# First-batch q and k pieces in one transfer each, adjacent heads in the halves of TensorE, and the last attention units spread 8, 8, 5 over the phases

## The chip, the cores and the metric

The kernel runs on one core of a Trainium2 chip. The metric is device time in microseconds (us), from the first to the last instruction of one execution. Each time quoted is the median of several executions. Ratios are computed otherwise: the mean time of one kernel's fast runs over the mean of the other's fast runs in the same rounds, so a ratio is not quite the ratio of two quoted medians. The interval behind a ratio is a 95% interval.

A run counts as slow when it is over 1.5% above the fastest of the same kernel; slow runs are in the medians but not in the ratios.

In the profiles PE is TensorE's matmuls, PEld its weight loads, DVE VectorE, ACT ScalarE, POOL GpSimd (it issues the loads) and SP SyncE (it issues the DMA transposes and the stores). PSUM is the memory that TensorE's results go to, in eight banks (`ps`).

## The reference

Windowed causal attention with a linear distance penalty feeds a two-matrix layer with a cosine gate. There are 8 batches (B), 8 heads (H), 576 tokens (S) and 64 values per head (D).

```python
scores = q @ k.transpose(0, 1, 3, 2) / sqrt(64)
rel = pos[:, None] - pos[None, :]
scores = where((rel >= 0) & (rel < 128), scores - slope[h] * rel, -1e9)
x = softmax(scores) @ v                    # -> 4608 tokens x 512
h = x @ w_in                               # 512 -> 2048
out = (h * cos(h)) @ w_out                 # 2048 -> 512
```

## The kernel before

The kernel works through nine chunks of 512 tokens, one per phase `c`. A phase issues the first product of its chunk (`moe1`: TensorE, cosine on ScalarE, multiply on VectorE), then some attention units for later chunks, then the second product (`moe2`). A unit is one pair of heads and 256 queries, or the tail of a batch. Nine units are a batch. The first nine run before the phases, and `QUOTA` says how many run in each phase after that: 9 + 9 + 9 + 12 + 12 + 12 + 9 = 72.

```python
NX = 8
xnat = [sb(f"xnat{i}", [128, 256]) for i in range(NX)]
...
QUOTA = [9, 9, 12, 12, 12, 9]
...
for c in range(NCH):                       # NCH = 9
    ...                                    # first product of chunk c
    n = QUOTA[c] if c < len(QUOTA) else 0
    attention(every[done:done + n], c)
    done += n
    ...                                    # next batches: load_v, load_nat, dma_transposes
    moe2(c)
```

A unit ends with a normalisation on VectorE, which writes a row buffer `xnat[n % NX]`, where `n` counts units. From there the rows go to `xT` by a transpose on TensorE if the next phase needs them, and otherwise by a DMA transpose that SyncE issues. The buffer is free when that transfer has landed. The first two batches use another pair of buffers (`xg`), which two units share.

```python
key = ("xnat", n % NX)
o = xnat[n % NX][:, :].rearrange("p (r x d) -> p r x d", r=2, x=2)
...
op("dve", ... o, U[:, :, :, 0:64], rv[...], ALU.mult ..., w=[("B", ub), key])
...
op("sp", [lambda e: e.dma_start_transpose(
    xT[:, pr, t0:t0 + 256].rearrange("p (r t) -> p r t", r=2), xnat[n % NX][:, :])],
   r=[("xnat", n % NX)], w=xkeys(pr, t0, 256), dma=f"x{n % NX}", occ=1250, lat=500)
```

Batches 0 and 1 bring q and k in rows and transpose them on TensorE. Batch 0 comes in two pieces (tokens 0 to 255, then 256 to 575), each in two transfers, because its heads stand four apart:

```python
def head(b, pr, x):
    return pr + 4 * x if b < BPE else 2 * pr + x
...
fns = [lambda e, y=y: e.dma_start(
    qB[which][:, y, c0:c0 + 64 * R],
    src[b, 4 * y:4 * y + 4, t0:t0 + 32 * R, :].rearrange(
        "k (s j) d -> s k (j d)", j=R)) for y in range(2)]
op("pool", fns, ..., occ=800 if b else 1260, lat=2900 if b else 170 * R)
```

`occ` and `lat` are assumed costs. A list schedule orders all instructions by them before anything is emitted. Each engine then runs its own list strictly in order.

The softmax here doesn't subtract the row's maximum and nothing guards it: scores larger than these inputs give would overflow.

## Time and profile before

| | the kernel before |
|---|---|
| time before the prediction, three runs | 324.82 us (323.61 to 326.19) |
| profile given at first | 1098.3 us span, TensorE at about a quarter of its speed |
| profile of the same kernel taken later (run `base`) | 323.9 us span |

### The profile page before, as it was taken

The numbers are of one execution on the slowest core, as the hardware profiler recorded it, in microseconds if no ns is written. First come the engines' busy times: TensorE is split into PE (matmuls) and PEld (weight loads), VectorE is DVE, ScalarE is ACT, GpSimd is POOL, SyncE is SP. The second block draws the span as 40 slices with busy tenths as digits, with TensorE's granted clock in tenths as the row PEclk, the third lists the DMA queues.
The fourth block names the chain that finished last, engine by engine and source line by source line (L and its number), as shares of the span: only waits on it lengthen the run. The fifth ranks groups of instructions, "written<-read, shape, count | busy, mean of one in ns | idle before, by whom it ended". The sixth has DMA issues, their size and how long they took to land.

```text
span 1098.3 us, 6162 instructions
## 1 busy us (share of the span) xinstructions
PE 1066.8 (97%) x2411; PEld 370.2 (34%) x2450; DVE 198.6 (18%) x420; ACT 209.5 (19%) x290; POOL 97.4 (9%) x127
## 2 busy tenths in 40 slices
PE   7999999999999999999999999999999999999998
PEld 4653342234223432343234422332222222222222
DVE  5220222112211222122212221311101110120000
ACT  5222212212222212121222121211101110110000
POOL 9300023011200120021000000000000000000000
DMA  9910249143901570185015000100000000000000
GB/s 156 181 13 0 46 52 85 29 38 42 73 10 15 72 50 8 21 83 65 3 31 70 17 0 10 33 8 0 10 10 19 0 10 19 10 0 20 19 28 20
DMA packets 144540, 37.82 MB, mean 34 GB/s; under 512 B 134272, under 2 KB 139392, under 8 KB 144512
## 3 DMA queue, kind: packets, MB, share of 16 engines
q0 software_dynamic: 99680, 18.36, 20.6%
q1 hardware_dynamic: 44832, 19.08, 7.3%
q8 instruction: 19, 0.31, 0.1%
q14 instruction: 9, 0.07, 0.0%
HBM read 36.70 MB, written 9.44 MB: 42 GB/s over the span
## 4 chain that ended last, share of the span: by engine, by line
PE 97%; issue 2%; POOL 0%; DMA 0%; DVE 0%; ACT 0%; POOLq 0%; ACTq 0%
PE ps L741 42%; PE ps L695 38%; PE ps L718 5%; PE ps L503 4%; PE ps L581 3%; PE ps L584 2%; PE ps L659 1%; PE ps L450 1%; PE ps L570 1%; PE ps L494 1%; PE ps L568 0%; DMA qrows<-in_q_dram 0%; POOL qrows L330 0%; POOL krows L330 0%; DVE xgroup L626 0%
## 5 line engine op out<-in xcount | busy, mean ns | idle before, releaser
L741 PE MATMUL ps<-w_outb,gT 128*128 128x512 bf16 x550 | 471.6, 1097 | 12.6 <-issue 11.6
L695 PE MATMUL ps<-xT,w_inb 128*128 128x512 bf16 x499 | 421.0, 1105 | 7.9 <-issue 7.9
L741 PEld LDWEIGHTS ps<-w_outb,gT 128*128 128x128 bf16 x576 | 115.7, 207 | 289.4 <-issue 289.4
L695 PEld LDWEIGHTS ps<-xT,w_inb 128*128 128x128 bf16 x512 | 111.9, 220 | 287.8 <-issue 277.6
L704 DVE TENSOR_TENSOR gT<-ps,cos 128x512 bf16<-128x512 f32 x128 | 87.4, 690 | 400.2 <-PE ps L741 200.9
L700 ACT ACTIVATE cos<-ps,halfpi 128x512 f32<-128x512 f32 x128 | 86.6, 687 | 349.4 <-PE ps L695 281.3
L533 ACT ACTIVATE p<-ps 128x768 bf16<-128x768 f32 (+1 forms) x64 | 55.9, 918 | 164.2 <-PE ps L503 150.7
L340 POOL DMA_DIRECT2D vp<-in_v_dram x40 | 33.8, 857 | 404.4 <-PE ps L584 356.4
L747 ACT ACTIVATE ob<-ps 128x512 f32<-128x512 f32 x26 | 15.5, 597 | 244.4 <-PE ps L741 226.5
L718 PE MATMUL ps<-xT,w_inb 128*128 128x256 bf16 x128 | 54.2, 684 | 0.0
L581 PE MATMUL ps<-vp,p 128*128 128x65 bf16 x256 | 53.1, 347 | 0.5 <-issue 0.5
L581 PEld LDWEIGHTS ps<-vp,p 128*128 128x128 bf16 x256 | 40.3, 181 | 24.1 <-issue 22.3
L549 DVE TENSOR_TENSOR p<-p,emask 128x768 bf16<-128x768 bf16 (+1 forms) x64 | 38.5, 615 | 54.6 <-ACT p L533 53.9
L503 PE MATMUL ps<-qt,kt 64*128 64x128 bf16 (+1 forms) x320 | 48.3, 508 | 0.0
L584 PE MATMUL ps<-vp,p 128*128 128x65 bf16 x192 | 46.2, 333 | 0.0
L503 PEld LDWEIGHTS ps<-qt,kt 64*128 64x128 bf16 x320 | 22.9, 160 | 46.9 <-issue 44.4
L624 DVE RECIPROCAL rec<-ps 128x4 f32<-128x4 f32 x64 | 8.3, 168 | 138.0 <-PE ps L584 138.0
L718 PEld LDWEIGHTS ps<-xT,w_inb 128*128 128x128 bf16 x128 | 25.4, 204 | 22.3 <-issue 22.0
L584 PEld LDWEIGHTS ps<-vp,p 128*128 128x128 bf16 x192 | 30.3, 171 | 7.7 <-issue 7.7
L350 POOL DMA_DIRECT2D knat<-in_k_dram x30 | 25.4, 901 | 74.4 <-DMA kt<-knat 73.1
L350 POOL DMA_DIRECT2D qnat<-in_q_dram x30 | 25.3, 887 | 7.0 <-DMA qt<-qnat 7.0
L749 DVE COPY ob<-ps 128x512 f32<-128x512 f32 x10 | 6.9, 692 | 66.4 <-PE ps L741 66.4
(56 smaller groups left out, 253.3 us busy)
## 6 DMA issues: line engine op xcount, KB each, us to landing
out_dram<-ob SPq DMA_DIRECT2D x36, 256.0 KB, 2.0
vp<-in_v_dram POOLq DMA_DIRECT2D x32, 128.0 KB, 4.6
qnat<-in_q_dram POOLq DMA_DIRECT2D x24, 128.0 KB, 4.1
knat<-in_k_dram POOLq DMA_DIRECT2D x24, 128.0 KB, 4.0
w_inb<-in_moe_w_in_dram POOLq DMA_DIRECT2D x4, 512.0 KB, 10.1
w_outb<-in_moe_w_out_dram POOLq DMA_DIRECT2D x4, 512.0 KB, 21.1
qrows<-in_q_dram POOLq DMA_DIRECT2D x1, 576.0 KB, 14.7
krows<-in_k_dram POOLq DMA_DIRECT2D x1, 576.0 KB, 16.5
```

What stands on the lines that cost most here:

```text
L340: op("pool", [lambda e, t=t, rows=rows: e.dma_start(vp[b % 2][0:rows, t, :, 0:64], v[b, :, 128 * t:128 * t + rows, :].rearrange("h p d -> ...
L350: fns.append(lambda e, t=t, rows=rows: e.dma_start(nat[which][0:rows, t, :, :], src[b, :, 128 * t:128 * t + rows, :].rearrange("h p d -> p ...
L503: ins = e.matmul(ps[:, banks[x], c0:c1], keys_ap(b, x, pr, kc), query_ap(b, x, pr, qb, 128 * nb), start=True, stop=True)
L533: op("act", lambda e: e.activation(P[i][:, :, lo:512], src_[:, :, lo:512], ACTF.Exp, scale=0.125), w=held + [("P", i)], occ=920 if G else ...
L549: op("dve", lambda e: e.tensor_tensor(P[i][:, :, lo:512], P[i][:, :, lo:512], EM[:, h0:h1 + 1:h1 - h0, lo:512], ALU.mult), r=[("P", i), (" ...
L581: ins = e.matmul(o, P[i][:, x, d0:d0 + 128], V[:, kc, h, 0:65], start=True, stop=not two)
L584: ins = e.matmul(o, P[i][:, x, p0:p0 + 128], V[:, kc - 1, h, 0:65], start=False, stop=True)
L695: op("pe", lambda e, kc=kc: e.matmul(ps[:, bank, :], w_in[:, kc, 128 * fc:128 * fc + 128], xT[:, kc, r0:r0 + CH], start=(kc == 0), stop=(k ...
L700: op("act", lambda e: e.activation(cosb[ci][:, :], ps[:, bank, :], ACTF.Sin, bias=halfpi[:, 0:1]), r=["halfpi"], w=[("B", bank), ("cos", c ...
L704: op("dve", lambda e: e.tensor_tensor(gT[gi][:, fc, :], ps[:, bank, :], cosb[ci][:, :], ALU.mult), r=[("cos", ci)], w=[("B", bank), ("g", ...
L718: op("pe", lambda e, i=i, fc=fc, kc=kc: e.matmul(ps[:, bank, 256 * i:256 * i + 256], w_in[:, kc, 128 * fc:128 * fc + 128], xT[:, kc, r0:r0 ...
L741: op("pe", lambda e, t=t, fc=fc, bank=bank: e.matmul(ps[:, bank, :], gT[gi][:, fc, 128 * t:128 * t + 128], w_out[:, fc, :], start=(fc == 0 ...
```

## The change

The intent: fewer transfers to issue at the start, so that TensorE gets its first pieces sooner; adjacent heads, so that one access pattern covers a piece and one tail mask and one kind of result buffer serve all batches; and phases with less attention.

```diff
-        QUOTA = [9, 9, 12, 12, 12, 9]
+        QUOTA = [9, 9, 12, 12, 8, 8, 5]
...
-        def head(b, pr, x):
-            return pr + 4 * x if b < BPE else 2 * pr + x
...
-            if b:
-                fns = [... one transfer ...]
-            else:
-                fns = [... two transfers, y = 0 and 1 ...]
-            op("pool", fns, w=piece_keys(which, b, n), dma=f"ld{which}{n}",
-               occ=800 if b else 1260, lat=2900 if b else 170 * R)
+            rows = bass.AP(src.tensor, src[b].offset + 64 * t0,
+                           [[64 * R, 32], [64 * S, H], [1, 64 * R]])
+            op("pool", [lambda e: e.dma_start(qB[which][:, :, c0:c0 + 64 * R], rows)],
+               w=piece_keys(which, b, n), dma=f"ld{which}{n}", occ=800, lat=161 * R)
...
-            if b < BPE:
-                key = ("xg", pr // 2, pr % 2)
-                o = xg[pr // 2][:, :, :, 64 * (pr % 2):64 * (pr % 2) + 64]
-            else:
-                key = ("xnat", n % NX)
-                o = xnat[n % NX][:, :].rearrange("p (r x d) -> p r x d", r=2, x=2)
+            key = ("xnat", n % NX)
+            o = xnat[n % NX][:, :].rearrange("p (r x d) -> p r x d", r=2, x=2)
```

Cut: the masks in head order, one tail mask instead of two, `2 * pr + x` for `head(...)` everywhere, and what follows from them in the transposes. With the quota, the phase c = 4 goes from 12 units to 8, c = 5 from 9 to 8, and c = 6 from none to 5.

The single transfer cannot be tried under the old pairing: a build of that failed, because its source then needs four dimensions ("Unable to balance aps with more than 3 dims"). That is why the pairing had to change with it.

More of the change, by code (lines that the diff above doesn't have):

```diff
@@ L266, in bass_alibi_sliding__then__act_gcu_kernel @@
         EM = sb("emask", [128, H, 512])
-        EMt = [sb(f"emtail{i}", [128, H, 128]) for i in range(2)]
-        xg = [sb(f"xgroup{i}", [128, 2, 2, 128]) for i in range(2)]
+        EMt = sb("emtail", [128, H, 128])
         NP = 4
@@ L324, in load_qk @@
             c0 = 64 * (t0 // 32)
-            if b:
-                fns = [lambda e: e.dma_start(
-                    qB[which][:, :, :],
-                    src[b].rearrange("(y k) (s j) d -> (k s) y (j d)", y=2, j=18))]
-            else:
-                fns = [lambda e, y=y: e.dma_start(
-                    qB[which][:, y, c0:c0 + 64 * R],
-                    src[b, 4 * y:4 * y + 4, t0:t0 + 32 * R, :].rearrange(
-                        "k (s j) d -> s k (j d)", j=R)) for y in range(2)]
-            op("pool", fns, w=piece_keys(which, b, n), dma=f"ld{which}{n}",
-               occ=800 if b else 1260, lat=2900 if b else 170 * R)
+            rows = bass.AP(src.tensor, src[b].offset + 64 * t0,
+                           [[64 * R, 32], [64 * S, H], [1, 64 * R]])
+            op("pool", [lambda e: e.dma_start(qB[which][:, :, c0:c0 + 64 * R], rows)],
+               w=piece_keys(which, b, n), dma=f"ld{which}{n}", occ=800, lat=161 * R)
         def load_v(b, order=range(NBLK)):
@@ L415, in masks @@
         def masks():
-            for h in (0, 4, 1, 5, 2, 6, 3, 7):
+            for h in range(H):
                 op("act", lambda e, h=h: e.activation(
@@ L420, in masks @@
                    table=0)
-                if h >= 4:
+                if h % 2:
                     op("dve", lambda e, h=h: e.tensor_copy(
-                        EM[:, h - 4:h + 1:4, 256:512], EM[:, h - 4:h + 1:4, 0:256]),
-                       r=[("EM", h - 4), ("EM", h)], w=[("EM", h - 4), ("EM", h)],
+                        EM[:, h - 1:h + 1, 256:512], EM[:, h - 1:h + 1, 0:256]),
+                       r=[("EM", h - 1), ("EM", h)], w=[("EM", h - 1), ("EM", h)],
                        occ=250, lat=330)
-            for i in range(2):
-                for x in range(2):
-                    hs = [head(BPE * i, pr, x) for pr in range(NPAIR)]
-                    op("dve", lambda e, i=i, x=x, hs=hs: e.tensor_copy(
-                        EMt[i][:, 4 * x:4 * x + 4, :].rearrange("p h (n f) -> p h n f", n=2),
-                        EM[:, hs[0]:hs[-1] + 1:hs[1] - hs[0], 0:256].rearrange(
-                            "p h (n f) -> p h n f", n=2)[:, :, :, 0:64]),
-                       r=[("EM", h) for h in hs], w=[("EMt", i)], occ=500, lat=580)
+            for x in range(2):
+                op("dve", lambda e, x=x: e.tensor_copy(
+                    EMt[:, 4 * x:4 * x + 4, :].rearrange("p h (n f) -> p h n f", n=2),
+                    EM[:, x:x + 7:2, 0:256].rearrange("p h (n f) -> p h n f", n=2)[:, :, :, 0:64]),
+                   r=[("EM", h) for h in range(x, H, 2)], w=["EMt"], occ=500, lat=580)
         def qk_transposes(b, which, n, part, banks):
@@ L460, in qk_transposes @@
                     :, :, t0:t0 + 32 * R].rearrange("p k (s j) -> p k s j", j=R)[:, :, :, j0:j1]
-                order = "p (j k s) -> p k s j" if b else "p (j s k) -> p k s j"
-                src_ = dst(i).rearrange(order, j=j1 - j0, k=NPAIR)
+                src_ = dst(i).rearrange("p (j s k) -> p k s j", j=j1 - j0, k=NPAIR)
                 w = 140 * (j1 - j0)
@@ L543, in mask @@
                     Pt[i][:, 0:1024], Pt[i][:, 0:1024],
-                    EMt[b >= BPE][:, :, :].rearrange("p h f -> p (h f)"), ALU.mult),
-                   r=[("Pt", i), ("EMt", int(b >= BPE))], w=[("Pt", i)], occ=610, lat=693, pri=1)
+                    EMt[:, :, :].rearrange("p h f -> p (h f)"), ALU.mult),
+                   r=[("Pt", i), "EMt"], w=[("Pt", i)], occ=610, lat=693, pri=1)
                 return
             lo = 0 if G else 128
-            h0, h1 = head(b, pr, 0), head(b, pr, 1)
+            h0, h1 = 2 * pr, 2 * pr + 1
             op("dve", lambda e: e.tensor_tensor(
                 P[i][:, :, lo:512], P[i][:, :, lo:512],
-                EM[:, h0:h1 + 1:h1 - h0, lo:512], ALU.mult),
+                EM[:, h0:h1 + 1, lo:512], ALU.mult),
                r=[("P", i), ("EM", h0), ("EM", h1)], w=[("P", i)],
@@ L564, in f @@
                             for k_ in range(NPAIR):
-                                h = head(b, k_, x)
+                                h = 2 * k_ + x
                                 o = ps[:, UB[x], 65 * k_:65 * k_ + 65]
@@ L574, in f @@
                         for x in range(2):
-                            h = head(b, pr, x)
+                            h = 2 * pr + x
                             o = ps[:, ub, 65 * (2 * rb + x):65 * (2 * rb + x) + 65]
@@ L604, in norm @@
                 rv = rc[0:64, 0:8].rearrange("p (x k) -> p x k", x=2)
-                o = (xt_[:, :].rearrange("p (x k d) -> p x k d", k=4, x=2) if b < BPE else
-                     xt_[:, :].rearrange("p (k x d) -> p x k d", k=4, x=2))
+                o = xt_[:, :].rearrange("p (k x d) -> p x k d", k=4, x=2)
                 op("dve", lambda e: e.reciprocal(rv, U[:, :, :, 64]),
@@ L650, in x_pe @@
             else:
-                kc = pr // 2 + 2 * (pr % 2) if b < BPE else pr
                 def f(e):
@@ L656, in f @@
                     for r in range(2):
-                        i = (xg[pr // 2][:, r, pr % 2, :] if b < BPE else
-                             xnat[n % NX][:, 128 * r:128 * r + 128])
-                        ins = e.transpose(dst[:, 128 * r:128 * r + 128], i, ident[:, :])
+                        ins = e.transpose(dst[:, 128 * r:128 * r + 128],
+                                          xnat[n % NX][:, 128 * r:128 * r + 128], ident[:, :])
                     return ins
                 t0 = S * b + 256 * G
-                o, i = xT[:, kc, t0:t0 + 256], dst
-                keys = xkeys(kc, t0, 256)
-                rk = ([("xg", pr // 2, 0), ("xg", pr // 2, 1)] if b < BPE else
-                      [("xnat", n % NX)])
+                o, i = xT[:, pr, t0:t0 + 256], dst
+                keys = xkeys(pr, t0, 256)
+                rk = [("xnat", n % NX)]
             op("pe", f, r=rk + ["ident"], w=[("B", bank)], occ=120, lat=290, pri=0)
```

## The prediction

> **What bounds the kernel now.** I read the page first (busy shares, the chain that ended last, the groups), then the timeline of the first 24 us and of the last 8, then half-microsecond stretches of the start with the DMA rate. The first thing to see is that the profile is not of an execution like the timed ones: its span is 1098.3 us, the timed runs took 324.82 us.
>
> ```profile
> span 1098.3 us, 6162 instructions
> ...
> PE 1066.8 (97%) x2411; PEld 370.2 (34%) x2450; DVE 198.6 (18%) x420; ACT 209.5 (19%) x290; POOL 97.4 (9%) x127
> ...
> DMA 9910249143901570185015000100000000000000
> ...
> L741 PE MATMUL ps<-w_outb,gT 128*128 128x512 bf16 x550 | 471.6, 1097 | 12.6 <-issue 11.6
> L695 PE MATMUL ps<-xT,w_inb 128*128 128x512 bf16 x499 | 421.0, 1105 | 7.9 <-issue 7.9
> L704 DVE TENSOR_TENSOR gT<-ps,cos 128x512 bf16<-128x512 f32 x128 | 87.4, 690 | 400.2 <-PE ps L741 200.9
> ```
>
> TensorE is busy 97%, and the matmul groups have next to no idle time before them. What pace it runs at is seen in the last microseconds of the timeline, from one weight load to the next:
>
> ```profile
> 1090.50 0.26 PEld L741 LDWEIGHTS ps<-w_outb,gT 128*128 128x128 bf16 x1 [0.58 <-issue]
> 1091.34 0.26 PEld L741 LDWEIGHTS ps<-w_outb,gT 128*128 128x128 bf16 x1 [0.58 <-issue]
> ...
> 1095.12 0.60 ACT L747 ACTIVATE ob<-ps 128x512 f32<-128x512 f32 x1 [12.69 <-PE ps L741]
> ```
>
> One matmul of 512 columns every 0.84 us is 0.61 columns per ns. The two matrix products need 1152 such matmuls (9 chunks x 64, twice; the first chunk's are cut in halves), which is 968 us at that pace. That cannot fit in 324.82 us, so the timed runs have a TensorE about four times as fast, although the record gives the granted clock as 1.00. I therefore use the trace for what does not depend on TensorE (issues, transfers, ScalarE, VectorE), and rescale TensorE by 4.
>
> Rescaled sum for a timed run: 1152 x 0.216 us (the pace of the TensorE page, below) = 249 us. The chain of waits gives lines 741, 695 and 718 together 84.2% of the span, and the other TensorE lines (scores, attention times values, transposes) 12.5%, or 137 us; less some 14 us that lie in the start, a quarter of the rest is 31 us. The start, until the first matmul of the first product, takes 23.7 us in the timeline, and the end (last copy and store) about 3.3 us. Together 307 us; some 18 us of 324.8 are left for switches, gaps at the ends of phases and waits for transfers. So TensorE bounds a timed run as well, at some 90%. ScalarE's 209.5 us and VectorE's 198.6 us, which I take as unchanged, are 64% and 61% of 324.8: beside TensorE, but not far off in phases with much attention.
>
> The start is where the engines wait. Its timeline:
>
> ```profile
> 1.34 1.24 POOL L330 DMA_DIRECT2D qrows<-in_q_dram  x2 [0.82 <-POOLq L856]
> 2.56 1.09 POOL L330 DMA_DIRECT2D krows<-in_k_dram  x2
> 3.60 0.27 POOL L384 MEMSET ident<- 128x128 bf16 x1
> 5.00 1.67 PE L450 MATMUL ps<-ident,qrows 128*64 128x128 bf16 x16 [5.00 <-DMA qrows<-in_q_dram]
> 5.68 1.12 POOL L330 DMA_DIRECT2D qrows<-in_q_dram  x2 [0.15 <-issue]
> 7.44 1.56 PE L450 MATMUL ps<-ident,krows 128*64 128x128 bf16 x16 [0.77 <-DMA krows<-in_k_dram]
> 7.81 4.35 POOL L340 DMA_DIRECT2D vp<-in_v_dram  x5
> 10.21 2.14 PE L450 MATMUL ps<-ident,qrows 128*64 128x128 bf16 x20 [1.21 <-DMA qrows<-in_q_dram]
> 13.39 2.15 PE L450 MATMUL ps<-ident,krows 128*64 128x128 bf16 x20
> 15.07 0.76 POOL L326 DMA_DIRECT2D qrows<-in_q_dram  x1
> ```
>
> TensorE waits for each of the four pieces in turn. GpSimd is busy issuing all that time, and the second pieces, the values and the weights stand behind the first issues. The stretches show that the transfers are not at their limit early on:
>
> ```profile
> 4.50:5.00 0.50, 0.00 (x1) 0.01 (x2) 0.00 (x0) 0.00 (x0) 0.35 (x2) 1.00 0.77 92
> 6.50:7.00 0.50, 0.17 (x2) 0.00 (x0) 0.40 (x2) 0.50 (x3) 0.50 (x2) 1.00 0.42 52
> 16.50:17.00 0.50, 0.50 (x9) 0.26 (x6) 0.00 (x0) 0.50 (x2) 0.50 (x2) 1.00 1.28 212
> ```
>
> The last number is GB/s landed: 92 and 52 around 5 and 7 us, against about 205 once the weights flow. From 8 to 57 us the queue is never empty.
>
> **What the Trainium skill says.** "TensorE: Matmul & The Clock Gate", section "Seeing it yourself", warns that the clock events are unreliable and that the gate has been seen stuck at a quarter; this trace agrees, 0.61 columns per ns beside a recorded 1.00. The same page, "Back-to-back issue gap", gives N/2.4 + 2.5 ns warm, 216 ns for 512 columns; the trace cannot confirm it, the timed total only fits it. "DMA: Bandwidth & Descriptors", "Rules for kernel authors", says to coalesce small transfers; the trace shows what that saves here in issue, 0.76 us for one three-dimensional load against 1.24 us for two. "ScalarE: Activation LUTs", "What ACT_TABLE_LOAD costs", gives about 1283 ns for the load plus a drain; the trace has 1283 ns in all of them.
>
> **The change part by part.**
>
> *One transfer per tensor and piece.* Eight issues of batch 0 become four. Each pair costs 1.24, 1.09, 1.12 and 1.11 us; one issue of the same three-dimensional kind costs 0.76 or 0.71 us (line 326, batch 1). I take 0.74: the constants and the second q piece start 0.86 us earlier (1.24 + 1.09 - 2 x 0.74), the values and all behind them 1.6 us earlier. It is not all gain: the first half of q now leaves with the second, at about 2.1 instead of 1.9 us, so the first piece lands between 0.4 us earlier and 0.3 us later than 5.00. The second k piece, now at 13.39, is the last wait of the start; I expect it 1.0 to 1.6 us earlier. From there on transposes, scores and exponentials are unchanged, and the queue from 8 us on is moved by about as much, so weights and batch 1 arrive earlier too. On the path: -1.3 us.
>
> *Heads (2k, 2k+1) in the halves.* The mask multiply reads two adjacent heads instead of two four apart: same elements, same 615 ns. Two copies of the tail mask of 369 ns go (0.74 us of VectorE), at about 13.2 us, when the first exponentials run: off the path, 0 to -0.1. The result of the first two batches no longer waits for two units to share a buffer, and rotates over eight buffers instead of two: fewer waits of transposes, -0.2. The eviction of batch 1's transposes reads with a step of 4 instead of 1 across rows, but runs over the same inner dimension: 0.
>
> *Attention 8, 8, 5 instead of 12, 9, 0.* The 21 units stay 21, in 11 groups both before (6 + 5) and after (4 + 4 + 3). There is one more pair of table switches, 2 x 1.28 us of ScalarE. In a phase of 12 units ScalarE has 16 x 0.69 (cosines) + 12 x 0.92 (exponentials) + 2 x 1.28 (tables) + about 3 x 0.6 (output copies) = 26.5 us, against TensorE's 2 x 13.8 + some 5 = 33. After the cosines, 12 exponentials, two tables and the copies need 15.4 us, plus the waits between groups; the second product and the attention give TensorE 13.8 + 5 = 19 us to fill them with. So 12 units are near the limit at the end of the phase, where 8 leave several us. I give this 0.5 to 1.5 us for the 12, and take back up to 0.5 for the extra phase with a table switch. On the path: -0.8 us.
>
> *Order.* Instruction order is set by a list schedule on assumed costs; new costs shuffle it everywhere. I give this no sign and 1 us.
>
> Sum: -1.3 - 0.3 - 0.8 = -2.4 us; 324.82 - 2.4 = 322.4 us, 0.7% less.
>
> **The rivals.** *Start hidden by the queue:* the first pieces are bound by transfer, not issue, and the weights and batch 1's values come no earlier. For it: the queue is full from 8 to 57 us, and the last quarter of w_out lands near 43 us, about when a fast TensorE would need it. Against it: 52 and 92 GB/s early. Time: 323.6. *Late attention costs:* the phase with 5 units puts two table loads and exponentials where TensorE had nothing but dense matmuls, and a gap of 1 to 2 us opens. For it: the phases after 5 have no waits now. Against it: 13.8 us of second product to fill with and only 5 x 1.02 + 2.56 = 7.7 us on ScalarE. Time: 325. *Phase ends cost more than I think:* up to 18 us are unaccounted for; if phases of 12 lose 3 to 4 us each, the change wins more. For it: ScalarE and VectorE above 60%. Against it: only one of the three such phases is thinned. Time: 319.5.
>
> **Range and chances.** The three runs before lie between 323.61 and 326.19, so a median moves by about 0.8 us by itself; the start adds 0.8, the phases 1.2, the order 1. In quadrature 1.9 us, so 8 in 10 is about +-2.5, stretched downward for the last rival: 319.2 to 324.9. Faster by over 2% needs under 318.3: 8%. Slower by over 2% needs over 331.3, for which nothing speaks: 2%.
>
> **What would show it.** Four issues of about 0.74 us for batch 0's q and k; the identity's memset near 2.8 instead of 3.60 us; waits of TensorE for the second pieces ending near 9 and 12 us; the first product's first matmul near 22.4 instead of 23.73 us; two table loads more; two tail-mask copies fewer; no late gap of TensorE in the seventh phase. If the second k piece lands later than 13 us, or one issue costs over 1 us, the first part is wrong. If the profile comes out slow again, its span says nothing of the gain, and only the start can be compared.

## More of the kernel before

The prediction shows the first profile. The second came with the experiments and is the one to compare. Its head, with busy time, share of the span and instructions of each engine:

```profile
span 323.9 us, 6162 instructions
...
PE 306.1 (94%) x2411; PEld 154.7 (48%) x2450; DVE 190.1 (59%) x420; ACT 202.7 (63%) x290; POOL 97.6 (30%) x127
...
PE   2699999999999999999999979999999999999995
```

TensorE (PE) bounds the kernel, as the prediction worked out from the slow profile (some 90%). The row of digits gives TensorE's busy tenths in 40 slices of 8.1 us. Apart from the start and the last slice it holds one 7, in the slice from 186 to 194 us. The slow profile could not show that one.

## The result

| | median of six runs | ratio |
|---|---|---|
| before | 326.10 us (323.61 to 327.63) | |
| after | 321.65 us (320.85 to 322.34) | 0.9872 (0.9828 to 0.9915) |

The kernel is 1.28% faster, about 4.2 us of 326.1. That is within 2%, as predicted, and 321.65 us lies in the predicted range. The gain is larger than the 2.4 us worked out, though: the kernel before also came out at 326.1 here, not 324.82. A later repeat gave 322.00 us against 325.72 (ratio 0.9899), so the gain is 3.3 to 4.2 us. Why it is larger is what the experiments are for.

The head of the page after, and the two costliest lines of the groups (line, engine, operation, output and input, count, busy time, mean ns, then idle time ahead of them and its releaser):

```profile
span 319.1 us, 6207 instructions
...
PE 306.3 (96%) x2450; PEld 152.9 (48%) x2450; DVE 187.5 (59%) x413; ACT 204.1 (64%) x297; POOL 95.8 (30%) x123
...
PE   2799999999999999999999999999999999999995
...
L714 PE MATMUL ps<-w_outb,gT 128*128 128x512 bf16 x576 | 138.8, 379 | 0.0
L668 PE MATMUL ps<-xT,w_inb 128*128 128x512 bf16 x512 | 116.8, 379 | 0.4 <-DVE xnat L604 0.3
```

TensorE is as busy as before, 306 us, in a span 4.8 us shorter, and the 7 in the middle of its row is gone. Line 714 is the old 741 (second product) and 668 the old 695 (first product). The mean of 379 ns is from start to modelled end, and matmuls overlap. The pace is read from the weight loads at the end, one line of the timeline (start, length, line, count):

```profile
312.05 3.34 PEld L714 LDWEIGHTS ps<-w_outb,gT 128*128 128x128 bf16 x16
```

The last of 16 loads takes about 0.1 us, so (3.34 - 0.10) / 15 = 0.216 us lie from one to the next. The fourfold TensorE that the prediction had to assume is there.

The start of the timeline, where each piece was to come earlier. Before (run `base`):

```profile
7.30 1.06 PE L450 MATMUL ps<-ident,krows 128*64 128x128 bf16 x16 [1.27 <-DMA krows<-in_k_dram]
...
9.95 1.28 PE L450 MATMUL ps<-ident,qrows 128*64 128x128 bf16 x20 [1.59 <-DMA qrows<-in_q_dram]
...
13.25 1.28 PE L450 MATMUL ps<-ident,krows 128*64 128x128 bf16 x20 [1.27 <-DMA krows<-in_k_dram]
...
19.94 0.61 PE L718 MATMUL ps<-xT,w_inb 128*128 128x256 bf16 x2
```

After:

```profile
1.33 0.83 POOL L321 DMA_DIRECT2D qrows<-in_q_dram  x1 [0.81 <-POOLq L829]
...
2.15 0.72 POOL L321 DMA_DIRECT2D krows<-in_k_dram  x1
...
2.87 0.22 POOL L371 MEMSET ident<- 128x128 bf16 x1
...
5.26 1.07 PE L434 MATMUL ps<-ident,qrows 128*64 128x128 bf16 x16 [5.26 <-DMA qrows<-in_q_dram]
...
6.54 1.07 PE L434 MATMUL ps<-ident,krows 128*64 128x128 bf16 x16 [0.21 <-DMA krows<-in_k_dram]
...
9.29 1.28 PE L434 MATMUL ps<-ident,qrows 128*64 128x128 bf16 x20 [1.69 <-DMA qrows<-in_q_dram]
...
11.62 1.28 PE L434 MATMUL ps<-ident,krows 128*64 128x128 bf16 x20 [0.30 <-ACT qt L448]
...
17.34 0.61 PE L691 MATMUL ps<-xT,w_inb 128*128 128x256 bf16 x4
```

Single issues cost 0.83 and 0.72 us, and the identity comes at 2.87 us. The first q piece is 0.3 us later (4.96 in `base`). The others are 0.76, 0.66 and 1.63 us earlier, and the first product starts 2.6 us earlier.

Part of this is not the issue but the transfer. These are half-microsecond stretches of the start (stretch, its length, busy time and count of TensorE, weight loads, VectorE, ScalarE, GpSimd, then granted clock, DMA share, GB/s). Before:

```profile
4.50:5.00 0.50, 0.04 (x2) 0.04 (x4) 0.00 (x0) 0.00 (x0) 0.35 (x2) 1.00 0.91 123
```

After:

```profile
4.50:5.00 0.50, 0.00 (x0) 0.00 (x0) 0.00 (x0) 0.22 (x1) 0.35 (x2) 1.00 1.26 205
```

A first piece is 8 heads x 256 tokens x 64 values x 2 bytes = 262,144 bytes. At 205 GB/s that is 1.28 us, and 1.28 us is also what lies between the first q and the first k piece now (5.26 to 6.54). Before it was 2.34 us.

To see where the rest went I kept an account from the trace. Every weight load stands for one matmul, and all 2450 are recorded. I added up the work ahead of each at the full-speed pace of its kind (0.216 us for 512 columns; scores, values and transposes likewise, 298.2 us in all) and subtracted it from the time at which the load started. What is left is time lost so far. "Start" is read after 14 us of work, in the first product, "fifth phase" at 165 to 170 us of work, in the phase c = 4, and "after it" at 180.

| time lost so far, us | start | fifth phase | after it | end |
|---|---|---|---|---|
| before (`base`) | 14.2 | 17.4 | 19.9 | 21.9 |
| after | 11.55 | 15.1 | 15.3 | 17.1 |
| difference | 2.6 | 2.3 | 4.6 | 4.8 |

So the gain of this pair of profiles comes from two places: the start, 2.6 us, and something in the fifth phase, 2.3 us. In the fifth phase before, the timeline has this. TensorE:

```profile
190.39 0.20 PE L581 MATMUL ps<-vp,p 128*128 128x65 bf16 x1 [1.05 <-DVE xnat L626]
...
193.10 0.19 PE L568 MATMUL ps<-vp,ptail 128*128 128x65 bf16 x1 [1.00 <-DVE xnat L626]
```

and VectorE:

```profile
189.91 0.42 DVE L626 TENSOR_TENSOR xnat<-ps,rec 128x256 bf16<-128x256 f32 x1 [1.28 <-DMA xT<-xnat]
191.38 0.42 DVE L626 TENSOR_TENSOR xnat<-ps,rec 128x256 bf16<-128x256 f32 x1 [1.04 <-DMA xT<-xnat]
```

and the chain of waits through that stretch (start, length, what):

```profile
183.96 7.39 DMA xT<-xnat
```

TensorE waits for VectorE, and VectorE waits to write a row buffer until the DMA transpose of the unit eight before has landed, 7.39 us after its issue. The landing is only half of the time for which the buffer was held. The two buffers had been written by 177.35 and 177.68 us, but SyncE, which issues in order, had the transposes of the next batch's q first:

```profile
175.88 4.83 SPq L359 DMA_TRANSPOSE qt<-qnat  x1
180.75 1.24 SPq L362 DMA_TRANSPOSE qt<-qnat  x1
182.12 1.17 SPq L682 DMA_TRANSPOSE xT<-xnat  x1
...
183.96 2.36 SPq L682 DMA_TRANSPOSE xT<-xnat  x1
```

So their own transposes were issued 4.8 and 6.3 us after the buffers were full and landed at 189.88 and 191.35 us: each buffer was held for 12.5 to 13.7 us. What issuing them ahead of q would bring, no run tried. VectorE's late write also frees the PSUM bank for TensorE's next values, and the masks of later units stand behind it in VectorE's list. Over the whole page the phase costs TensorE the 7 in its row. The DMA view of 170 to 190 us gives the same landing time for these transposes after the change as before (count, median us):

```profile
xT<-xnat SPq DMA_TRANSPOSE x3, 7.6
```

Only nobody waits for them there. Two of them landed at 186.62 and 186.87 us, and the units that write these two buffers next now come in the phase after. VectorE after, at the same units, without a wait:

```profile
204.36 0.76 DVE L604 TENSOR_TENSOR xnat<-ps,rec 128x256 bf16<-128x256 f32 x2
```

### The profile page after: what moved, and what is told of

It is laid out like the page before. It is cut to its first block, busy times and chain, and to the rows that moved or that the text cites.

```text
span 319.1 us, 6207 instructions
## 1 busy us (share of the span) xinstructions
PE 306.3 (96%) x2450; PEld 152.9 (48%) x2450; DVE 187.5 (59%) x413; ACT 204.1 (64%) x297; POOL 95.8 (30%) x123
## 4 chain that ended last, share of the span: by engine, by line
PE 90%; DMA 6%; POOL 1%; issue 1%; DVE 0%; ACT 0%; POOLq 0%; ACTq 0%
PE ps L714 40%; PE ps L668 35%; DMA qrows<-in_q_dram 6%; PE ps L486 5%; PE ps L564 3%; PE ps L691 2%; PE ps L567 2%; PE ps L434 1%; PE ps L632 1%; PE ps L477 1%; PE ps L551 1%; PE ps L553 1%; POOL w_inb L357 1%; POOL qrows L321 0%; POOL krows L321 0%
## 5 line engine op out<-in xcount | busy, mean ns | idle before, releaser
L714 PE MATMUL ps<-w_outb,gT 128*128 128x512 bf16 x576 | 138.8, 379 | 0.0
L668 PE MATMUL ps<-xT,w_inb 128*128 128x512 bf16 x512 | 116.8, 379 | 0.4 <-DVE xnat L604 0.3
L714 PEld LDWEIGHTS ps<-w_outb,gT 128*128 128x128 bf16 x576 | 53.7, 98 | 58.7 <-issue 1.9
L668 PEld LDWEIGHTS ps<-xT,w_inb 128*128 128x128 bf16 x512 | 47.2, 98 | 61.2 <-DVE gT L677 6.0
L604 DVE TENSOR_TENSOR xnat<-ps,rec 128x256 bf16<-128x256 f32 x64 | 24.4, 420 | 0.7 <-DVE rec L602 0.4
L486 PE MATMUL ps<-qt,kt 64*128 64x128 bf16 (+1 forms) x320 | 19.0, 243 | 0.7 <-ACT p L516 0.7
L602 DVE RECIPROCAL rec<-ps 128x4 f32<-128x4 f32 x64 | 8.2, 168 | 18.1 <-PE ps L567 17.8
L564 PEld LDWEIGHTS ps<-vp,p 128*128 128x128 bf16 x256 | 15.4, 97 | 7.0 <-issue 3.5
L564 PE MATMUL ps<-vp,p 128*128 128x65 bf16 x256 | 18.2, 193 | 0.2 <-DVE p L532 0.2
L486 PEld LDWEIGHTS ps<-qt,kt 64*128 64x128 bf16 x320 | 11.2, 95 | 12.4 <-issue 5.1
L567 PE MATMUL ps<-vp,p 128*128 128x65 bf16 x192 | 17.0, 193 | 0.0
L691 PE MATMUL ps<-xT,w_inb 128*128 128x256 bf16 x128 | 16.0, 273 | 0.3 <-ACT xT L641 0.3
L567 PEld LDWEIGHTS ps<-vp,p 128*128 128x128 bf16 x192 | 13.3, 97 | 0.6
## 6 DMA issues: line engine op xcount, KB each, us to landing
qrows<-in_q_dram POOLq DMA_DIRECT2D x1, 576.0 KB, 15.1
krows<-in_k_dram POOLq DMA_DIRECT2D x1, 576.0 KB, 17.1
```

The costliest lines, as they stand in the source:

```text
L486: ins = e.matmul(ps[:, banks[x], c0:c1], keys_ap(b, x, pr, kc), query_ap(b, x, pr, qb, 128 * nb), start=True, stop=True)
L564: ins = e.matmul(o, P[i][:, x, d0:d0 + 128], V[:, kc, h, 0:65], start=True, stop=not two)
L567: ins = e.matmul(o, P[i][:, x, p0:p0 + 128], V[:, kc - 1, h, 0:65], start=False, stop=True)
L604: op("dve", lambda e: e.tensor_tensor(o, U[:, :, :, 0:64], rv[:, :, :, None].broadcast_to([128, 2, 2, 64]), ALU.mult), r=[("rec", n % 2)], ...
L668: op("pe", lambda e, kc=kc: e.matmul(ps[:, bank, :], w_in[:, kc, 128 * fc:128 * fc + 128], xT[:, kc, r0:r0 + CH], start=(kc == 0), stop=(k ...
L714: op("pe", lambda e, t=t, fc=fc, bank=bank: e.matmul(ps[:, bank, :], gT[gi][:, fc, 128 * t:128 * t + 128], w_out[:, fc, :], start=(fc == 0 ...
```

## The experiments

**Theory A** (from the profiles): the gain is two separate things, the start and the row buffers of the phase with 12 units. **Rival B** (from the prediction): the phase term comes from ScalarE at the end of a phase, so more buffers do nothing. **Rival C**: the list schedule's new order does it, or a colder TensorE clock at the start. **Rival D**: the pairing of heads has its own share.

The first four runs shared one chip and took the change apart. The kernel before came out at 325.78 us there.

**`base`**: the kernel before, unchanged, as a control.

> The kernel before, unchanged: ratio 1.00. It is run for a profile in the fast state. My theory (start 1.3 us, phases 0.8 us): the first matmul of the first product starts about 1.3 us later than the 17.34 us of the changed kernel, and TensorE shows some idle time at the ends of the phases with 12 units, 0.5 to 1.5 us in the fifth. Rival (all of the gain at the start): TensorE is without gaps from 20 us on, as in the changed kernel, and the first product starts 3 to 4 us later. Rival (reshuffled order): start and phases look alike and the difference is spread over many small pieces.

Measured: 325.60 us, ratio 0.9961 (0.9916 to 1.0006). The control is 0.4% from 1 by itself, so a ratio that is under half a per cent from another is not read alone.

**`quota_alone`**: the kernel before with the new quota.

```diff
-        QUOTA = [9, 9, 12, 12, 12, 9]
+        QUOTA = [9, 9, 12, 12, 8, 8, 5]
```

> Only the units per phase are changed (8, 8, 5 for 12, 9), the loads and heads are those of before. My theory: 0.8 us faster, ratio 0.9975. Rival that all of the gain is at the start: 1.000. Rival that thick phases cost more: 3 us faster, 0.990.

Measured: 323.01 us, ratio 0.9910 (0.9862 to 0.9958), 2.6 us under the control by medians. The account shows no loss through the fifth phase (16.5 us before and after it, against 17.4 and 19.9 in `base`). Its start differs by 1.6 us from that of `base` though the code of the start is the same, so profiles of single executions scatter by that much there. The time is what the rival "thick phases cost more" gave (0.990), not the 0.9975 of the theory.

**`whole_old_quota`**: the changed kernel with the old quota.

```diff
-        QUOTA = [9, 9, 12, 12, 8, 8, 5]
+        QUOTA = [9, 9, 12, 12, 12, 9]
```

> The changed kernel with the old units per phase (12, 9): one transfer per tensor and the new heads alone. My theory: 1.6 us of start and heads remain, ratio 0.995. Rival that all of the gain is at the start: 0.987, the whole. Rival that thick phases cost more: 0.996 to 1.000.

Measured: 325.87 us, ratio 0.9979 (0.9929 to 1.0030). Everything but the quota is worth nothing by itself. The account says where it went: the start is 2.1 us better (12.05), and the fifth phase loses 4.4 us (15.4 to 19.8) instead of 2.5. The hole became one wait of 3 us. TensorE and VectorE:

```profile
188.93 0.24 PE L564 MATMUL ps<-vp,p 128*128 128x65 bf16 x1 [3.00 <-DVE p L532]
```

```profile
187.52 0.76 DVE L604 TENSOR_TENSOR xnat<-ps,rec 128x256 bf16<-128x256 f32 x2 [2.81 <-DMA xT<-xnat]
```

After it the granted clock is 0.64 from 188 to 190 us and 0.50 from 190 to 192, where `base` has 1.00, so this profile loses more than the length of the wait. Whether the wait brings the lower clock on, no run tested; without the wait (`old_quota_nx12`, below) it stays at 1.00. The earlier start brings TensorE to this place 3.4 us sooner (it runs dry at 185.93 instead of 189.34 us), while the first of the two transfers lands only 2.4 us sooner (187.50 instead of 189.88).

**`two_transfers`**: the changed kernel, but with two transfers for each piece of batch 0, still in the new pairing (alternate heads in the two halves).

```diff
+            fns = [lambda e, y=y: e.dma_start(
+                qB[which][:, y, c0:c0 + 64 * R],
+                bass.AP(src.tensor, src[b].offset + 64 * t0 + 64 * S * y,
+                        [[64 * R, 32], [2 * 64 * S, 4], [1, 64 * R]])) for y in range(2)]
...            # with occ=1260, lat=170 * R for batch 0
```

> The changed kernel with two transfers per tensor and piece for batch 0 again (each takes every second head), with the issue cost of before given to the schedule; new heads and new units per phase. My theory: it loses the 1.3 us of the start, ratio 0.991 where the whole change has 0.987. Rival that the transfers are hidden by the queue anyway: 0.987 as the whole. Rival that all of the gain is the one transfer: 1.000.

Measured: 323.45 us, ratio 0.9921 (0.9880 to 0.9963), within 0.5 us of `quota_alone`: the pairing of heads with its removed copies and buffers is worth nothing that can be seen here. Against the whole change (0.9872 and 0.9899, in other rounds), the two transfers cost 0.2 to 0.5%, some 0.7 to 1.6 us, though the intervals overlap. The start is back as it was: first pieces at 5.02 and 7.32 us, the second q piece at 10.00 us, 111 GB/s in the stretch from 4.5 to 5 us. So the faster landing belongs to the single transfer, not to the order of heads.

The next four runs, on another chip (kernel before 324.99 us), put theory A against its rivals.

**`base_nx12`**: the kernel before with 12 row buffers. The order of instructions on every engine is the same as with 8 (the traces agree).

```diff
-        NX = 8
+        NX = 12
```

> The kernel before with 12 buffers for the attention rows instead of 8; the order of instructions on every engine is the same. Buffer theory (in the fifth phase VectorE waits for a row buffer whose DMA transpose stands behind the transpose of keys): both holes of TensorE near 188 and 191 us, 2.7 us together, go; 2.7 us faster, ratio 0.992. ScalarE theory of the prediction (12 units are too much for ScalarE at the end of a phase): the holes stay, 1.000.

Measured: 322.80 us, ratio 0.9946 (0.9925 to 0.9968), somewhat less than the 2.7 us expected. This one number takes 2.2 us out of the kernel before by medians, without touching the quota, ScalarE's work or the order. VectorE at the same place:

```profile
189.31 0.76 DVE L626 TENSOR_TENSOR xnat<-ps,rec 128x256 bf16<-128x256 f32 x2
```

No wait stands ahead of it, and the account runs level through the phase (18.1, 18.2). Rival B falls: 12 units in a phase are not too many for ScalarE. One thing in the expectation is not exact. It says that the slow transposes stand behind the transposes of the keys. In the queue's own list they are issued earlier (183.96 us, the keys' at 186.76); it is the transposes of q that stand ahead of them. Around that time the transpose of q takes 9.8 us to land and v's loads 9.4 us, so all transfers are slow there. Which of them slows the others no run separated.

**`old_quota_nx12`**: the changed kernel with the old quota and 12 row buffers.

```diff
-        NX = 8
+        NX = 12
-        QUOTA = [9, 9, 12, 12, 8, 8, 5]
+        QUOTA = [9, 9, 12, 12, 12, 9]
```

> The changed kernel with the old units per phase and 12 row buffers; order of instructions the same as with 8. Buffer theory: the hole of 3.2 us near 185 us and the slow clock after it go, about 4.6 us in all, and the gain of the start becomes visible: ratio 0.987, as the whole change. ScalarE theory: 0.998 as with 8 buffers.

Measured: 321.51 us, ratio 0.9909 (0.9889 to 0.9929), short of the 0.987 of the buffer theory but far from the 0.998 of its rival. The new quota isn't needed once there are buffers. And against `base_nx12` on the same chip, 322.80 - 321.51 = 1.3 us is what the start (with pairing and order) is worth when the hole isn't there to eat it.

**`costs_alone`**: the kernel before with the new assumed costs, so only the order of instructions changes, on TensorE in 646 lines; the transfers stay two per piece.

```diff
-               occ=800 if b else 1260, lat=2900 if b else 170 * R)
+               occ=800, lat=161 * R)
```

> The kernel before, with only the assumed costs of the first loads set to the changed kernel's: the same transfers and units, but the list schedule orders the instructions anew (646 lines of difference on TensorE). Theory of transfers and buffers: within 0.4% of the kernel before, 0.997 to 1.003, as long as the hole in the fifth phase stays. Rival that reshuffled order made the gain: 0.990 or less.

Measured: 326.47 us, ratio 1.0043 (1.0015 to 1.0070). This order by itself makes the kernel slower by 1.4 us; its profile has a wait of its own of 1.64 us, until 119.46 us, for a transpose of k. So the new costs alone do not make the gain. The changed kernel's own order, which the pairing and the quota shape too, was not tried alone. An order can cost over a microsecond, and the 1.3 us of the start contain a change of order.

**`early_pieces`**: the changed kernel with the second pieces issued right after the identity, ahead of the rest of the constants (an iota and two selections).

```diff
         constants()                        # now only the identity and the memsets
         load_qk("q", q, 0, 1)
         load_qk("k", k, 0, 1)
+        distances()                        # iota and two selections
         load_v(0)
```

> The changed kernel with the second q and k pieces issued ahead of the distance constants (iota and two selects), behind the identity alone. The second q piece is issued at about 3.5 instead of 4.90 us. Theory that the start is bound by the issue of the pieces: it lands near 8 instead of 9.29 us, and 1.0 to 1.3 us are gained over the changed kernel, ratio 0.983. Rival that the transfers bound it by now: lands no earlier than 9 us, ratio 0.987.

Measured: 321.57 us, ratio 0.9897 (0.9869 to 0.9926), no different from the whole change. The issue came 1.5 us earlier and the piece 0.6 us later (9.29 in the whole change):

```profile
3.42 0.76 POOL L321 DMA_DIRECT2D qrows<-in_q_dram  x1
...
9.87 1.28 PE L437 MATMUL ps<-ident,qrows 128*64 128x128 bf16 x20 [2.17 <-DMA qrows<-in_q_dram]
```

From issue to use it takes 6.45 us instead of 4.39. From there on, then, the second pieces are bound by the transfer and not by the issue.

The last four runs, on a third chip (kernel before 325.72 us), tested the clock and looked for a better version. In the fast profiles TensorE is slow at the start though the record says 1.00: in `base`, matmuls of scores with values lie 54 to 56 ns apart up to 22.64 us and 29 from 22.73 on; in the profile after they are 29 apart from 13.59 us on. An earlier full clock was therefore a rival for the start's gain.

**`base_warm`** and **`whole_warm`**: the kernel before and the changed one with throw-away transposes of the identity ahead of TensorE's four waits for pieces (6, 12, 16, 14 and 14, 3, 17, 5), outside the schedule, so that the order is unchanged. Shown for the changed one:

```diff
+        WARM = {'q0': 14, 'k0': 3, 'q1': 17, 'k1': 5}
...
+                def pre(e):                # emitted ahead of the waits for batch 0's pieces
+                    for _ in range(WARM[f"{which}{n}"]):
+                        e.transpose(spare psum bank, ident[:, :], ident[:, :])
```

> The kernel before with throw-away transposes of the identity (6, 12, 16 and 14) ahead of TensorE's four waits for q and k pieces; all other instructions in the same order. Clock theory: in the kernel before TensorE runs at half rate until 16 to 22 us because it idles so much in the start; kept busy, it reaches the full rate by 9 us, the scores near 16 us go at 36 instead of 60 ns, and 1.5 to 2 us are gained: ratio 0.994. Rival (only the landings matter): 1.000, or slower by the throw-away work that outlasts a wait, up to 1.003.

> The changed kernel with throw-away transposes (14, 3, 17, 5) ahead of the same four waits. Clock theory: the full rate comes at about 8 instead of 13 us, which shortens the second pieces' transposes and the first scores: 0.5 to 1 us less than the changed kernel of the same call. Rival: the same time within 0.3 us.

**`whole_again`**: the changed kernel once more, as the control.

> The changed kernel once more, beside the others of this call: ratio 0.987 to 0.991.

Measured: `base_warm` 329.80 us, ratio 1.0046 (0.9988 to 1.0103), with three of six runs slow and left out of the ratio; `whole_again` 322.00 us, 0.9899 (0.9857 to 0.9941); `whole_warm` 322.29 us, 0.9903 (0.9865 to 0.9942). With the throw-away work TensorE was at its full pace (transposes 56 ns apart) by 9.8 us in `base_warm` and 7.8 in `whole_warm`, and the first product came no sooner: at 19.81 us (19.94 in `base`) and at 18.45 (17.34 to 18.40 in three profiles of the changed kernel, one of them with 12 buffers). The times alone would not tell, since both had longer waits for row buffers later (4.8 and 2.2 us in all, against 2.3 and none). What the first product waits for once TensorE is quick is the weights. `base_warm`, then `whole_warm`:

```profile
19.81 0.54 PE L731 MATMUL ps<-xT,w_inb 128*128 128x256 bf16 x2 [1.33 <-DMA w_inb<-in_moe_w_in_dram]
```

```profile
18.45 0.61 PE L704 MATMUL ps<-xT,w_inb 128*128 128x256 bf16 x4 [1.18 <-DMA w_inb<-in_moe_w_in_dram]
```

So the clock theory of the start falls. With both kernels bound by the landing of w_in, the change brings the first product 19.81 - 18.45 = 1.36 us earlier, in one profile each. All fast profiles together give a firmer measure. The first quarter of w_in lands at 19.01 to 20.22 us in the six with two transfers per piece (`base`, `quota_alone`, `two_transfers`, `base_nx12`, `costs_alone`, `base_warm`) and at 17.21 to 18.40 us in the seven with one, on average 1.8 us earlier and without overlap. Pairing, quota and order vary among the six, quota and order among the seven. The first product starts 0.04 to 0.38 us after it in all of them. In `base_warm` the holes of the fifth phase grew to 1.36 and 3.14 us; why they did is open.

**`whole_nx12`**: the changed kernel with 12 row buffers.

```diff
-        NX = 8
+        NX = 12
```

> The changed kernel with 12 row buffers. Buffer theory: with 8, 8 and 5 units no wait for a row buffer is left on the path, so this changes nothing: within 0.3 us of the changed kernel. If buffers still bound it somewhere: 0.5 us or more faster.

Measured: 320.51 us (320.30 to 321.00), ratio 0.9846 (0.9814 to 0.9878), the best of all, and 1.5 us under `whole_again` on the same chip. This is a miss of the theory (no wait for a row buffer left, within 0.3 us) and what its alternative gave. One short wait of VectorE is gone. In `whole_again`, then in `whole_nx12`:

```profile
182.59 0.75 DVE L604 TENSOR_TENSOR xnat<-ps,rec 128x256 bf16<-128x256 f32 x2 [0.39 <-DVE rec L602]
```

```profile
181.87 0.76 DVE L604 TENSOR_TENSOR xnat<-ps,rec 128x256 bf16<-128x256 f32 x2
```

That explains 0.4 us in the profile, and the accounts end 0.7 us apart (17.9 and 17.2). The rest of the 1.5 us is not located. A hint: the new quota does not end the waits for row buffers in every execution. The profiles of `early_pieces` and `whole_warm`, with 8 buffers, have such waits of VectorE near 155 us, of 0.92 us and of 0.81 and 1.38 us, at the last two units of the phase c = 3, which still has 12. Executions without a profile may have them too; no run shows it.

## Why the prediction was right or wrong

The class and the range were right, and the change came out somewhat better than its sum. By its steps:

**TensorE as the bound, from a slow profile.** Right. The rescaling by 4 gave 0.216 us per matmul, and the fast profiles have that. The 18 us that were left over for switches, gaps and waits were where the second half of the gain lay: the slow profile could not show which phase they belong to, because at a quarter of the speed the transfers are in time: its normalisations to `xnat` idle 0.5 us in all, and in `base` 2.8 us, of which 2.3 for the DMA transposes.

**One transfer per tensor and piece, -1.3 us.** Right in size, in part by luck. With the hole out of the way the measured value is 1.3 us (`base_nx12` to `old_quota_nx12`, with order and pairing in it); undoing the transfers alone costs 0.7 to 1.6 us (`two_transfers`), and the first quarter of w_in lands 1.8 us earlier on average. The prediction took the second k piece for the last wait of the start; in the fast profiles the first product starts right after that quarter of w_in. That fits the step that the prediction named, the earlier issue of all that stands behind (batch 1's q at 13.52 instead of 15.17 us, 1.65 earlier where 1.6 was said). The marks hold: single issues of 0.83, 0.72, 0.75 and 0.71 us, the identity at 2.87 us, the first q piece 0.3 us later, the second ones at 9.29 and 11.62 us. Two more points were missing from the working. The transfer itself became faster (205 instead of 123 GB/s; 1.28 instead of 2.34 us from piece to piece; the cause isn't settled), and the term does not show by itself: under the old quota it was lost again in the fifth phase (`whole_old_quota`, 0.9979 beside a control of 0.9961).

**Heads, -0.3 us.** Not seen: `two_transfers` (0.9921) has the new heads and no gain over `quota_alone` (0.9910). The two tail copies did go.

**Attention 8, 8, 5, -0.8 us.** This is the step that failed: it was mis-sized, and its reason was wrong. The prediction said "12 units are near the limit at the end of the phase", meaning ScalarE. It measured 2.6 us (`quota_alone` against `base`), and 2.2 us came from four more row buffers alone (`base_nx12`), with ScalarE's work untouched. The limit was the number of row buffers, 8, against 12 units and a buffer that was held for over 12 us, 5 to 6 of them ahead of the issue of its transpose and over 7 from there to the landing. The kernel's text showed the 8 and the 12. What the prediction left out was to ask, for each buffer that rotates, how long its release takes and how many units run in that time; it took waits on `xg` into account, and not those on `xnat`, which it counted as a gain.

**Order, no sign, 1 us.** About right: `costs_alone` is 1.4 us slower by order alone.

**The rivals.** "Start hidden by the queue" is true of the second pieces beyond what the change did (`early_pieces`), and not of the change. "Late attention costs" is refuted: the seventh phase has no gap, and the two table loads more (16 instead of 14, 1283 ns each) cost nothing visible. "Phase ends cost more than I think" came nearest, 319.5 us, with a loss of 2.2 to 2.6 us per thinned phase where it said 3 to 4; but it happens within the phase, and by another cause.

With the terms as measured, 1.3 + 2.6 = 3.9 us, which fits the 3.3 to 4.2 us of the two pairs of runs. That 321.65 us lies so near the 322.4 worked out is in part luck: the gain was larger, but the three runs at first had put the kernel before at 324.82 us, 1.3 us under the median of six.

## What to carry to other kernels

Where an engine writes into buffers that a transfer must free, compare the number of buffers with the units that are written while one buffer is held, before blaming an engine's throughput. That time runs from the write to the landing: here 5 to 6 us in the issuing engine's list, behind other transfers, and over 7 us on the way. An in-order engine that waits for such a buffer holds up everything listed behind it, and a gain made earlier can vanish whole in that wait; so test parts with the later wait taken away as well. Two things that seem to be alternatives, thinner phases and more buffers, can be cures of the same wait; trying the cheaper one by itself tells.

## What the Trainium skill lacked or had wrong

- "TensorE: Matmul & The Clock Gate", section "Seeing it yourself", has the gate stuck at a quarter for 50 us and more. Here a whole execution of 1098.3 us ran at that pace (0.61 columns per ns) with a recorded clock of 1.00, and fast executions began at about half of full pace (in `base` 54 to 56 ns from one matmul with values to the next up to 22.64 us, later 29) with the record at 1.00 as well.
- No page, as far as was looked, says how long a DMA transpose takes to land beside other traffic (it would belong to "DMA: Bandwidth & Descriptors"). Here the one that freed a row buffer took 7.39 us, the median of such transposes between 170 and 190 us was 7.6 us in both kernels, and between 100 and 170 us it was 4.6 us in the kernel before.
